# Gated linear attention with a mixture of adapters: the order and the rings of the input loads

## The chip, the cores and the metric

The kernel runs on one core of one Trainium2 chip. The metric is device time in microseconds (us) of one execution. Before the change three timed runs gave a median of 113.31 us (113.30 to 113.52). Five engines work side by side: TensorE (PE) for matmuls, VectorE (DVE), ScalarE (ACT), GpSimd (POOL) and SyncE (SP). Transfers between device memory and on-chip memory are issued as instructions on the SP or the ACT queue, each of which feeds a ring of its own, and are carried out by 16 DMA engines that both rings share.

## The reference

Two stages follow each other. The first is a recurrence over 768 time steps, for 4 batches of 8 heads, with a 48 by 48 state for each head:

```python
for t in range(S):
    state = alpha[:, :, t, :, None] * state + np.einsum('bhd,bhe->bhde', k[:, :, t], v[:, :, t])
    y[:, :, t] = np.einsum('bhd,bhde->bhe', q[:, :, t], state)
```

The second takes y as 3072 tokens of 384 features, picks the two best of eight experts for each token, and adds a rank-16 correction:

```python
logits = x @ w_gate                                   # 384 x 8
topk = np.argpartition(-logits, K, axis=1)[:, :K]     # K = 2
w = exp(sel - max) / sum                              # sel: the two chosen logits
delta[mask] += w[mask, k, None] * (x[mask] @ A[e]) @ B[e]
return x + delta
```

Inputs q, k, v and alpha are float32, 4 x 8 x 768 x 48 each: 4.72 MB each, 18.87 MB together. The adapter weights add 0.4 MB. The output is 4.72 MB.

## The kernel before

The time steps are cut into chunks of 128, so each batch has 6 chunks and there are 24 units (`NU`), numbered u = 6 b + c. One unit is 128 time steps on the partitions, with all 8 heads (384 numbers) along the row. Each input of one unit is one DMA of 192 KB (L290). In device memory a head's row is 48 floats, so this DMA is made of 1024 pieces of 192 bytes.

For one unit the work goes through these operations. The short names are those that the planner uses, and the line numbers are those of the profile.

- `ln` (L374, ACT): logarithm of alpha. Units 0 and 1 are done alone, then two units share one instruction (`LNS`), so `ln` of units 2 and 3 needs the alpha of both.
- `cum` (L379 to L385, PE): sums of the logarithms along time. `exp` (L390, ACT): their exponentials.
- `kg` (L395, POOL): k and q times the exponentials. `vb` (L403, POOL): v cast to bf16.
- `tr` (L409, PE): transposes. `kq` (L413, ACT): copy out of PSUM. `at` (L421, PE): scores. `msk` (L426, DVE): causal mask.
- `st` (L433, DVE) and `kv` (L441, L446, PE): the state carried from chunk to chunk. `av` (L456, L463, PE): the chunk's y. It needs `vb`.
- `ysb` (L468, ACT), `xt` (L481, PE), `xs` (L486, ACT): y copied out, transposed, copied out again.

Every three units (`GROUPS`; the last groups are [21, 22] and [23]) the adapter stage runs: `z` (L500, PE), the gate operations `gm`, `df`, `ge`, `gx`, `wu`, `dn`, `w` (L507 to L542, DVE but for `gx` on ACT), `zw` (L549, DVE), `zt` (L558, PE), `zs` (L564, ACT), and for each unit `dl` (L569, PE) and `o` (L577, DVE). The finished unit is stored by one DMA from SP (L600).

The order of instructions on each engine is fixed when the kernel is built. A list scheduler (`_order`) simulates the engines with assumed durations (`_ops`), assumed arrival times of the inputs (`_arrivals`) and a priority for each kind of operation (`PRIO`), and the instructions are written out in the order that it finds. On the chip each engine takes its instructions in that order and waits at each until its inputs are there.

The loads are ordered by `_plan`: for each unit alpha, k, q, v, in this order. `_ring` spreads them: of the first six the odd ones go to ACT, after that every fourth, which is always v. So SP carries 73 of the 99 loads (with the three weight loads) and ACT 26. SP issues nothing but DMAs. Its loads are written out by `pump`, and as SP does no other work it runs ahead until its ring has no room or a buffer is not free (each input has buffers for two batches, so the load for unit u needs the reading of unit u - 12 to be over). A load on ACT is an operation of the planner (`ld`), due `LEAD` = 5 us before its assumed arrival, and stands among ACT's other work, in order.

The weights are loaded on SP in a row, behind the first 20 input loads (L298 to L301). Three casts on DVE (`cast_weights`, L340 to L343) turn them into bf16. They are written out just before `xs` of unit 0. Stores are written out only once all loads have been.

Of the kernel before, what the change touches and what calls it, by code (L numbers as in the profile page):

```python
# [16 lines left out]
B, H, S, D = 4, 8, 768, 48  # L17
C = 128
# [14 lines left out]
LNS = [[0], [1]] + [[u, u + 1] for u in range(2, NU, 2)]  # L33
CAST = set()
LEAD = 5.
FIRST = 6


def _ring(i, item):
    return "ACT" if (i % 2 if i < FIRST else i % 4 == 3) else "SP"  # L40

def _act(n):
# [15 lines left out]
def _pe(t):  # L62
    return t + .22, t
# [2 lines left out]
SMALL = (.2, .09)  # L66
KEEP = dict(lg=2, ex=3, kg=4, kt=4, am=3, sb=2, vb=4, xs=9)
SLOTS = dict(C=1, A=1, M=3)
PRIO = dict(ln=-27.4, cum=-33.5, exp=14.2, kg=-6.0, vb=0.6, tr=4.7, kq=-8.2, at=6.7, msk=15.1,
            st=25.4, kv=6.9, av=-15.0, ysb=22.1, xb=5.9, xt=12.5, xs=-29.2, z=13.2, gm=32.7,  # L70
            df=16.8, ge=17.3, gx=21.3, wu=-9.0, dn=-22.2, w=39.9, zw=20.3, zt=1.9, zs=21.7,
            dl=6.9, o=21.2)
PERIOD = 2.0
SLACK = 0


def _plan():
    plan = []
    for u in range(NU):
        b, c = divmod(u, NCH)  # L80
        plan += [(x, b, c) for x in "akqv"]
    return plan


def _arrivals(plan):
    t, arr = 2.6, {}
    for i, (x, b, c) in enumerate(plan):
        t += 4.2 if c is None else .75
        for j in (range(NCH) if c is None else (c,)):
            arr[x, b * NCH + j] = t  # L90
        arr["due", i] = t - LEAD
    return arr


def _ops(arr):
    ops = {}

    def add(name, eng, length, deps, war=(), alloc=None, frees=None):
        ops[name] = (eng, length, list(deps), list(war), alloc, frees)

    gof = {u: g for g, us in enumerate(GROUPS) for u in us}
    lof = {u: us for us in LNS for u in us}
    prev = []
    for i, (x, b, c) in enumerate(_plan()):
        if i >= FIRST and _ring(i, (x, b, c)) == "ACT":
            war = []
            for j in (range(NCH) if c is None else (c,)):
                u = (b - 2) * NCH + j
                if u >= 0:
                    war.append(dict(a=("ln", lof[u][0]), k=("kg", u), q=("kg", u), v=("vb", u))[x])  # L110
            add(("ld", i), "ACT", (.5, .45), [("due", i)], war + prev)
            prev = [("ld", i)]
    for i, us in enumerate(LNS):
        war = [("cum", u) for u in LNS[i - KEEP["lg"]]] if i >= KEEP["lg"] else []
        add(("ln", us[0]), "ACT", _act(DM * len(us) + 30), [("a", u) for u in us], war)
    for u in range(NU):
        c = u % NCH
        p = u - KEEP["ex"]
        add(("cum", u), "PE", _pe(.49), [("ln", lof[u][0])], alloc="C")
        add(("exp", u), "ACT", _act(776), [("cum", u)],  # L120
            [("kg", p)] + ([("st", p)] if p % NCH else []), frees=("cum", u))
        p = u - KEEP["kg"]
        add(("kg", u), "POOL", _gp(768), [("exp", u), ("k", u), ("q", u)],
            [("tr", p)] + ([("kv", p)] if p % NCH < NCH - 1 else []))
        add(("vb", u), "POOL", _gpc(DM), [("v", u)], [("av", u - KEEP["vb"])])
        add(("tr", u), "PE", _pe(.48), [("kg", u)], alloc="M")
        add(("kq", u), "ACT", _act(512), [("tr", u)], [("av", u - KEEP["kt"])], frees=("tr", u))
        add(("at", u), "PE", _pe(.40), [("kq", u)], alloc="A")
        add(("msk", u), "DVE", _dve(1024), [("at", u)], [("av", u - KEEP["am"])], frees=("at", u))
        if c:  # L130
            add(("st", u), "DVE", _dve(DM), [("kv", u - 1), ("exp", u)], [("av", u - KEEP["sb"])])
        if c < NCH - 1:
            add(("kv", u), "PE", _pe(.33 if c else .17),
                [("vb", u), ("kg", u)] + ([("st", u)] if c else []),
                [] if c or not u else [("st", u - 1)])
        add(("av", u), "PE", _pe(.49 if c else .32),
            [("msk", u), ("vb", u), ("kq", u)] + ([("st", u)] if c else []), alloc="M")
        add(("ysb", u), "ACT", _act(DM), [("av", u)], frees=("av", u))
        if u in CAST:
            add(("xb", u), "POOL", _gpc(DM), [("ysb", u)])  # L140
            add(("xt", u), "PE", _pe(.17), [("xb", u)], alloc="M")
        else:
            add(("xt", u), "PE", _pe(.38), [("ysb", u)], alloc="M")
        p = u - KEEP["xs"]
        add(("xs", u), "ACT", _act(DM), [("xt", u)], [("z", gof[p])] if p >= 0 else [],
            frees=("xt", u))
    for g, us in enumerate(GROUPS):
        n = len(us)
        add(("z", g), "PE", _pe(.18 * n), [("xs", u) for u in us], alloc="M")
        add(("gm", g), "DVE", (.17 + .13 * (n - 1), .13 * n), [("z", g)])  # L150
        add(("df", g), "DVE", SMALL, [("gm", g)])
        add(("ge", g), "DVE", SMALL, [("gm", g)])
        add(("gx", g), "ACT", _act(E * n), [("df", g)])
        add(("wu", g), "DVE", SMALL, [("gx", g), ("ge", g)])
        add(("dn", g), "DVE", SMALL, [("wu", g)])
        add(("w", g), "DVE", (.4, .29), [("dn", g)])
        add(("zw", g), "DVE", _dve(P * n), [("w", g)], frees=("z", g))
        add(("zt", g), "PE", _pe(.057 * n), [("zw", g)], alloc="M")
        add(("zs", g), "ACT", _act(64 * n), [("zt", g)], frees=("zt", g))
        for u in us:  # L160
            add(("dl", u), "PE", _pe(.165), [("zs", g)], alloc="M")
            add(("o", u), "DVE", _dve(DM), [("dl", u)], frees=("dl", u))
    return ops
# [76 lines left out]
def kernel(  # L240
# [36 lines left out]
    def home(x, b):  # L277
        i = b % 2
        return dict(a=a_t[i], k=kq_t[i][:, 0], q=kq_t[i][:, 1], v=v_t[i])[x]

    def view(t):
        return t.rearrange("p (h c) d -> p c h d", h=H)[:, :, :, 0:D]

    def load(item, eng):
        x, b, c = item
        t, src = home(x, b), SRC[x][b]
        if c is None:
            eng.dma_start(out=t[:, :, 0:D], in_=src.rearrange("h (c j) d -> j (h c) d", j=C))
        else:
            eng.dma_start(out=view(t)[:, c],  # L290
                          in_=src[:, c * C:(c + 1) * C, :].rearrange("h j d -> j h d"))
# [5 lines left out]
    def load_weights():  # L297
        nc.sync.dma_start(out=W_st.rearrange("p e i r -> p e (i r)"),  # L298
                          in_=moe_A.rearrange("e (p i) r -> p e (i r)", i=NF))
        nc.sync.dma_start(out=G_st, in_=moe_w_gate.rearrange("(p i) e -> p i e", i=NF))  # L300
        nc.sync.dma_start(out=B_st, in_=moe_B.rearrange("e r f -> (e r) f"))  # L301

    queue = list(enumerate(plan))
    for i in range(FIRST):
        load(queue.pop(0)[1], nc.sync if _ring(i, plan[i]) == "SP" else nc.scalar)
    rings = {r: [x for x in queue if _ring(*x) == r] for r in ("SP", "ACT")}

    suf = consts.tile([P, P], F2, name="suf")
    nc.gpsimd.memset(suf, 1.0)
# [260 lines left out]
                         start=True, stop=True)  # L570

    def ld(i):
        assert rings["ACT"][0][0] == i
        load(rings["ACT"].pop(0)[1], nc.scalar)

    def o(u):
        nc.vector.tensor_tensor(out=o_t[u], in0=bank("dl", u)[:, 0:DM], in1=o_t[u], op=ALU.add)  # L577
# [6 lines left out]
    weights = 20  # L584
    done = []

    def pump(now):
        q = rings["SP"]
        while q:
            i, (x, b, c) = q[0]  # L590
            if arr["due", i] > now or any(
                    (b - 2) * NCH + j not in reads[x]
                    for j in (range(NCH) if c is None else (c,)) if b > 1):
                return
            load(q.pop(0)[1], nc.sync)

    def store(u):
        b, c = divmod(u, NCH)
# [2 lines left out]

    with tc.manual_schedule():
        for s, i in order:
            if (s, i) == ("xs", 0):
                cast_weights()
            RUN[s](i)
            for x, r in READ.items():
                if r == s:
                    for u in (LNS[lof[i][0]] if s == "ln" else (i,)):
                        reads[x].add(u)  # L610
            pump(when[s, i][0])
            if weights and len(plan) - len(rings["SP"]) - len(rings["ACT"]) >= weights:
                load_weights()
                weights = None
            if s == "o":
                done.append(i)
            if not rings["SP"] and not rings["ACT"]:
                while done:
                    store(done.pop(0))

# [29 lines left out]
```

## Time and profile before

| what | value |
|---|---|
| median of three timed runs | 113.31 us |
| the profiled execution's own time | 113.9 us |
| its span, first to last instruction | 112.2 us |
| mean granted TensorE clock | 0.906 of full speed |
| read from device memory / written | 19.28 MB / 4.72 MB |
| last alpha (unit 23) landed | 87.1 us |
| last load issued on SP | 83.63 to 86.27 us |
| first store issued, last `o` starts | 86.4 us, 108.7 us |

All times are microseconds from the first instruction of the profiled execution. Outside the span lie 1.7 us (113.9 less 112.2). The busy time of an engine is an average over stages with different limits, so the stretches from the profile that the prediction shows matter more than the totals. "Idle before, releaser" beside a group of instructions tells how long the engine stood still just before them and what it waited for. A name that ends in q (SPq, ACTq) is an engine's queue: the time that it spends on issuing a DMA is not counted as busy.

### The profile page before, as it was taken

Reading aid. Unit: us, or ns where it says so; the run is one execution under the profiler, and the core shown is the slowest. Engines: PE = TensorE matmul, PEld = TensorE weight load, DVE = VectorE, ACT = ScalarE, POOL = GpSimd, SP = SyncE. Lnnn points to the kernel's source line nnn. Section 1 sums busy time; section 2 is a strip of 40 time slices with the busy share of each in tenths; the row PEclk is TensorE's granted clock in tenths of the full one; section 3 lists DMA queues with packets and bytes.
Section 4 is the critical chain, followed back from the end, with each engine's and each line's share of the span. In section 5 each row is a group of like instructions: output and inputs, shape, how many; then the busy total and the mean of one; then the engine's idle time right before and its main releaser. Section 6 shows DMA issues by size and latency. Waiting matters only on the chain.

```text
span 112.2 us, 2916 instructions
## 1 busy us (share of the span) xinstructions
PE 80.6 (72%) x1112; PEld 62.2 (55%) x1112; DVE 69.1 (62%) x170; ACT 66.2 (59%) x128; POOL 56.2 (50%) x58
## 2 busy tenths in 40 slices
PE   0346994099995496978947969899395699996540
PEld 0124863067874286856836748579283478974210
DVE  4004330765595287899575396967289265998990
ACT  4244476046973767967818769696592745754310
POOL 5077418605949278492691676839287076000000
PEclk9999999558999999999997699999999656999975
DMA  2999999899999899999989999999899999013064
GB/s 57 259 259 259 259 230 275 181 224 212 247 240 185 165 256 237 220 244 205 230 173 214 256 241 187 246 243 229 175 259 191 338 394 390 9 72 141 3 235 186
DMA packets 104638, 24.19 MB, mean 216 GB/s; under 512 B 101424, under 2 KB 104624, under 8 KB 104624
## 3 DMA queue, kind: packets, MB, share of 16 engines
q1 hardware_dynamic: 77584, 18.89, 74.4%
q10 hardware_dynamic: 27040, 5.11, 22.7%
q8 instruction: 8, 0.13, 0.5%
q14 instruction: 6, 0.05, 0.2%
HBM read 19.28 MB, written 4.72 MB: 214 GB/s over the span
## 4 chain that ended last, share of the span: by engine, by line
SPq 39%; DMA 18%; PE 16%; DVE 16%; issue 4%; ACT 3%; DVEq 1%; POOL 1%; ACTq 0%; POOLq 0%
SPq L290 37%; DMA a_t<-in_alpha_dram 18%; DVE am L426 5%; DVE o_t L577 3%; ACT lg L374 3%; PE M_t L409 2%; PE cum_t L379 2%; DVE zw L549 2%; PE M_t L481 2%; DVE w L542 2%; PE at_t L421 2%; PE cum_t L380 1%; PE M_t L456 1%; SPq L300 1%; SPq L298 1%
## 5 line engine op out<-in xcount | busy, mean ns | idle before, releaser
L395 POOL TENSOR_TENSOR kgq<-kq_t,ex 128x768 bf16<-128x768 f32 x24 | 43.6, 1818 | 29.4 <-ACT ex L390 29.4
L426 DVE TENSOR_TENSOR am<-at_t,mask 128x1024 bf16<-128x1024 f32 x24 | 29.3, 1221 | 8.9 <-PE at_t L421 8.8
L390 ACT ACTIVATE ex<-cum_t 128x776 f32<-128x776 f32 x24 | 19.7, 822 | 5.8 <-PE cum_t L385 5.4
L379 PE MATMUL cum_t<-lg,suf 128*128 128x384 bf16 x24 | 9.0, 377 | 16.1 <-ACT lg L374 15.8
L374 ACT ACTIVATE lg<-a_t 128x768 bf16<-128x768 f32 (+1 forms) x13 | 10.3, 795 | 15.9 <-DMA a_t<-in_alpha_dram 15.9
L433 DVE TENSOR_TENSOR sb<-S_t,ex 128x384 bf16<-128x384 f32 x20 | 11.0, 551 | 13.1 <-PE S_t L446 8.7
L409 PE MATMUL M_t<-ident,kgq 128*128 128x128 bf16 x192 | 16.9, 238 | 2.7 <-POOL kgq L395 2.2
L413 ACT COPY kqt<-M_t 128x512 f32<-128x512 f32 x24 | 14.0, 584 | 8.0 <-PE M_t L409 7.7
L403 POOL CAST vb<-v_t 128x384 bf16<-128x384 f32 x24 | 12.0, 509 | 8.7 <-PE M_t L463 5.9
L409 PEld LDWEIGHTS <-kgq 128*128 128x128 bf16 x192 | 12.8, 107 | 4.9 <-POOL kgq L395 3.1
L577 DVE TENSOR_TENSOR o_t<-M_t,o_t 128x384 f32<-128x384 f32 x24 | 12.5, 551 | 3.6 <-PE M_t L569 3.4
L481 PE MATMUL M_t<-ident,o_t 128*128 128x128 f32 x72 | 14.1, 315 | 0.4 <-ACT o_t L468 0.4
L486 ACT CAST xs<-M_t 128x384 bf16<-128x384 f32 x24 | 11.2, 480 | 3.5 <-PE M_t L481 2.6
L468 ACT COPY o_t<-M_t 128x384 f32<-128x384 f32 x24 | 11.6, 483 | 1.9 <-PE M_t L463 1.9
L380 PEld LDWEIGHTS <-nsuf 128*128 128x128 bf16 x24 | 2.5, 105 | 15.5 <-issue 15.3
L481 PEld LDWEIGHTS M_t<-ident,o_t 128*128 128x128 f32 x72 | 10.2, 203 | 1.1 <-ACT o_t L468 0.9
L421 PE MATMUL at_t<-kqt 48*128 48x128 bf16 x192 | 10.6, 236 | 0.4 <-ACT kqt L413 0.4
L463 PE MATMUL M_t<-vb,am 128*128 128x48 bf16 x192 | 9.3, 189 | 0.3 <-DVE am L426 0.3
L446 PEld LDWEIGHTS <-kgq 128*128 128x128 bf16 x80 | 6.4, 110 | 5.2 <-issue 4.3
L380 PE MATMUL cum_t<-lg,nsuf 128*128 128x384 bf16 x24 | 9.2, 384 | 0.0
L441 PE MATMUL S_t<-sb,ident 128*128 128x384 bf16 x16 | 5.9, 370 | 3.5 <-DVE sb L433 3.5
L569 PE MATMUL M_t<-B_all,zs 128*128 128x384 bf16 x24 | 7.1, 338 | 1.3 <-DVE o_t L577 0.5
(47 smaller groups left out, 102.1 us busy)
## 6 DMA issues: line engine op xcount, KB each, us to landing
a_t<-in_alpha_dram SPq DMA_DIRECT2D x24, 192.0 KB, 4.3
kq_t<-in_q_dram SPq DMA_DIRECT2D x24, 192.0 KB, 4.4
v_t<-in_v_dram ACTq DMA_DIRECT2D x24, 192.0 KB, 4.0
out_dram<-o_t SPq DMA_DIRECT2D x24, 192.0 KB, 2.5
kq_t<-in_k_dram SPq DMA_DIRECT2D x22, 192.0 KB, 4.5
kq_t<-in_k_dram ACTq DMA_DIRECT2D x2, 192.0 KB, 4.3
W_st<-in_moe_A_dram SPq DMA_DIRECT2D x1, 192.0 KB, 4.6
B_st<-in_moe_B_dram SPq DMA_DIRECT2D x1, 192.0 KB, 4.0
```

The lines of the kernel that those rows point to most:

```text
L290: eng.dma_start(out=view(t)[:, c], in_=src[:, c * C:(c + 1) * C, :].rearrange("h j d -> j h d"))
L374: nc.scalar.activation(lgs[i % KEEP["lg"]][:, 0:n, :, 0:D], view(a_t[b % 2])[:, c:c + n], AF.Ln)
L380: nc.tensor.matmul(cum_t[:, N0:D0], nsuf[:, :], t[:, :, 0:D], start=True, stop=True)
L390: nc.scalar.activation(st["ex"][u], cum_t[:, U0:D0 + 2 * NP], AF.Exp)
L395: nc.gpsimd.tensor_tensor(out=kgq[u % KEEP["kg"]][:, :, :, 0:D], in0=src, in1=st["ex"][u][:, 0:2 * DM].rearrange("p (w h d) -> p w h d", w ...
L403: nc.gpsimd.tensor_copy(out=st["vb"][u], in_=view(v_t[b % 2])[:, c])
L409: nc.tensor.transpose(t[:, w, p, :], pair(kgq[u % KEEP["kg"]][:, w], p), ident[:, :])
L413: nc.scalar.copy(t, bank("tr", u)[:, :])
L421: nc.tensor.matmul(at_t[:, hh, p, :], kq[rows, 0, p, :], kq[rows, 1, p, :], start=True, stop=True)
L426: nc.vector.tensor_tensor(out=st["am"][u].rearrange("p a b t -> p (a b) t"), in0=at_t.rearrange("p a b t -> p (a b) t"), in1=_bc_mid(mask[ ...
L481: nc.tensor.transpose(t[:, i * P:(i + 1) * P], x[:, i, :], idn[:, :])
L577: nc.vector.tensor_tensor(out=o_t[u], in0=bank("dl", u)[:, 0:DM], in1=o_t[u], op=ALU.add)
```

## The change

The list of loads is reordered, spread over the rings in another way, and written out in another way. The order and priorities of all other work come from the same planner with other numbers.

- `_plan` now starts a0, k0, q0, a1, v0, k1, q1, a2, a3, v1. After that each unit brings k and q, each even unit u also alpha of units u + 2 and u + 3, then v of the unit. The four weight loads (A in two halves) follow unit 3. The v of units 22 and 23 are the last two loads.
- `_ring` is strict alternation: even places on SP, odd places on ACT, weights included. That is 50 loads on each. Of the 100, the first eight (`FIRST`) are written out ahead of all other work, four on each ring.
- An `ld` on ACT keeps its due time of 5 us before the assumed arrival. The planner now books 0.1 us of ACT for it instead of 0.45 us. The loads of SP that lie between are written out with it; `pump` is gone. A load writes out when the buffer's earlier reading has been written out.
- `cast_weights` is written out just before `z` of group 0 instead of `xs` of unit 0.
- Assumed arrivals start at 2.9 us and come every 0.77 us (0.4 us for a weight load), where they started at 2.6 us and came every 0.75 us. All `PRIO` numbers, some PE durations and `SLACK` (0.05 us instead of 0) are new.

```diff
-FIRST = 6
-def _ring(i, item):
-    return "ACT" if (i % 2 if i < FIRST else i % 4 == 3) else "SP"
+FIRST = 8
+def _ring(i):
+    return "ACT" if i % 2 else "SP"
...
-PRIO = dict(ln=-27.4, cum=-33.5, exp=14.2, kg=-6.0, vb=0.6, tr=4.7, kq=-8.2, at=6.7, msk=15.1,
-            st=25.4, kv=6.9, av=-15.0, ysb=22.1, xb=5.9, xt=12.5, xs=-29.2, z=13.2, gm=32.7,
-            df=16.8, ge=17.3, gx=21.3, wu=-9.0, dn=-22.2, w=39.9, zw=20.3, zt=1.9, zs=21.7,
-            dl=6.9, o=21.2)
+PRIO = dict(ln=-64.4, cum=-19.5, exp=15.9, kg=-34.5, vb=36.9, tr=-5.5, kq=18.9, at=0.3, msk=25.2,
+            st=17.2, kv=6.3, av=-46.4, ysb=38.7, xb=6.2, xt=35.6, xs=-33.5, z=16.2, gm=44.4,
+            df=23.7, ge=23.8, gx=22.6, wu=-24.6, dn=-0.6, w=-22.4, zw=15.5, zt=-8.7, zs=-7.1,
+            dl=8.4, o=21.5)
-SLACK = 0
+SLACK = 0.05
 def _plan():
-    plan = []
-    for u in range(NU):
-        b, c = divmod(u, NCH)
-        plan += [(x, b, c) for x in "akqv"]
-    return plan
+    plan = [("a", 0), ("k", 0), ("q", 0), ("a", 1), ("v", 0), ("k", 1), ("q", 1), ("a", 2), ("a", 3), ("v", 1)]
+    for u in range(2, NU):
+        plan += [("k", u), ("q", u)]
+        if u % 2 == 0 and u + 2 < NU:
+            plan += [("a", u + 2), ("a", u + 3)]
+        if u < NU - 2:
+            plan += [("v", u)]
+        if u == 3:
+            plan += [("w", 0), ("w", 1), ("w", 2), ("w", 3)]
+    return plan + [("v", NU - 2), ("v", NU - 1)]
 def _arrivals(plan):
-    t, arr = 2.6, {}
-    for i, (x, b, c) in enumerate(plan):
-        t += 4.2 if c is None else .75
+    t, arr = 2.9, {}
+    for i, x in enumerate(plan):
+        t += .4 if x[0] == "w" else .77
...
-            add(("ld", i), "ACT", (.5, .45), [("due", i)], war + prev)
+            add(("ld", i), "ACT", (.4, .1), [("due", i)], war + prev)
...
-        add(("cum", u), "PE", _pe(.49), [("ln", lof[u][0])], alloc="C")
+        add(("cum", u), "PE", _pe(.52), [("ln", lof[u][0])], alloc="C")
...
+    A_src = moe_A.rearrange("e (p i) r -> p e (i r)", i=NF)
+    WSRC = ((W_st[:, 0:4].rearrange("p e i r -> p e (i r)"), A_src[:, 0:4]),
+            (W_st[:, 4:8].rearrange("p e i r -> p e (i r)"), A_src[:, 4:8]),
+            (G_st, moe_w_gate.rearrange("(p i) e -> p i e", i=NF)),
+            (B_st, moe_B.rearrange("e r f -> (e r) f")))
+    loaded = 0
+    def load_next():
+        nonlocal loaded
+        x, u = plan[loaded]
+        eng = nc.sync if _ring(loaded) == "SP" else nc.scalar
+        loaded += 1
+        if x == "w":
+            eng.dma_start(out=WSRC[u][0], in_=WSRC[u][1])
+            return
+        b, c = divmod(u, NCH)
+        eng.dma_start(out=view(home(x, b))[:, c],
+                      in_=SRC[x][b][:, c * C:(c + 1) * C, :].rearrange("h j d -> j h d"))
+    while loaded < FIRST:
+        load_next()
...
     def ld(i):
-        assert rings["ACT"][0][0] == i
-        load(rings["ACT"].pop(0)[1], nc.scalar)
+        assert loaded <= i
+        while loaded <= i or (loaded < len(plan) and _ring(loaded) == "SP" and free(loaded)):
+            load_next()
+    def free(i):
+        x, u = plan[i]
+        return u < 2 * NCH or u - 2 * NCH in reads[x]
...
-            if (s, i) == ("xs", 0):
+            if (s, i) == ("z", 0):
                 cast_weights()
             RUN[s](i)
...
-            pump(when[s, i][0])
-            if weights and len(plan) - len(rings["SP"]) - len(rings["ACT"]) >= weights:
-                load_weights()
-                weights = None
             if s == "o":
                 done.append(i)
-            if not rings["SP"] and not rings["ACT"]:
+            if loaded == len(plan):
                 while done:
                     store(done.pop(0))
```

More of the change, by code (lines that the diff above doesn't have):

```diff
@@ L68 @@
 SLOTS = dict(C=1, A=1, M=3)
-PRIO = dict(ln=-27.4, cum=-33.5, exp=14.2, kg=-6.0, vb=0.6, tr=4.7, kq=-8.2, at=6.7, msk=15.1,
-            st=25.4, kv=6.9, av=-15.0, ysb=22.1, xb=5.9, xt=12.5, xs=-29.2, z=13.2, gm=32.7,
-            df=16.8, ge=17.3, gx=21.3, wu=-9.0, dn=-22.2, w=39.9, zw=20.3, zt=1.9, zs=21.7,
-            dl=6.9, o=21.2)
+PRIO = dict(ln=-64.4, cum=-19.5, exp=15.9, kg=-34.5, vb=36.9, tr=-5.5, kq=18.9, at=0.3, msk=25.2,
+            st=17.2, kv=6.3, av=-46.4, ysb=38.7, xb=6.2, xt=35.6, xs=-33.5, z=16.2, gm=44.4,
+            df=23.7, ge=23.8, gx=22.6, wu=-24.6, dn=-0.6, w=-22.4, zw=15.5, zt=-8.7, zs=-7.1,
+            dl=8.4, o=21.5)
 PERIOD = 2.0
-SLACK = 0
+SLACK = 0.05
 def _plan():
-    plan = []
-    for u in range(NU):
-        b, c = divmod(u, NCH)
-        plan += [(x, b, c) for x in "akqv"]
-    return plan
-def _arrivals(plan):
-    t, arr = 2.6, {}
-    for i, (x, b, c) in enumerate(plan):
-        t += 4.2 if c is None else .75
-        for j in (range(NCH) if c is None else (c,)):
-            arr[x, b * NCH + j] = t
+    plan = [("a", 0), ("k", 0), ("q", 0), ("a", 1), ("v", 0), ("k", 1), ("q", 1), ("a", 2), ("a", 3), ("v", 1)]
[8 more added lines that the diff above has]
+    return plan + [("v", NU - 2), ("v", NU - 1)]
+def _arrivals(plan):
+    t, arr = 2.9, {}
+    for i, x in enumerate(plan):
+        t += .4 if x[0] == "w" else .77
+        arr[x] = t
         arr["due", i] = t - LEAD
@@ L102, in _ops @@
     lof = {u: us for us in LNS for u in us}
[L103 to L110, printed above, removed]
-            add(("ld", i), "ACT", (.5, .45), [("due", i)], war + prev)
-            prev = [("ld", i)]
+    war, prev = [], []
+    for i, (x, u) in enumerate(_plan()):
+        if u >= 2 * NCH:
+            p = u - 2 * NCH
+            war.append(dict(a=("ln", lof[p][0]), k=("kg", p), q=("kg", p), v=("vb", p))[x])
+        if i >= FIRST and _ring(i) == "ACT":
+            add(("ld", i), "ACT", (.4, .1), [("due", i)], war + prev)
+            war, prev = [], [("ld", i)]
     for i, us in enumerate(LNS):
@@ L125, in _ops @@
         add(("vb", u), "POOL", _gpc(DM), [("v", u)], [("av", u - KEEP["vb"])])
-        add(("tr", u), "PE", _pe(.48), [("kg", u)], alloc="M")
+        add(("tr", u), "PE", _pe(.5), [("kg", u)], alloc="M")
         add(("kq", u), "ACT", _act(512), [("tr", u)], [("av", u - KEEP["kt"])], frees=("tr", u))
-        add(("at", u), "PE", _pe(.40), [("kq", u)], alloc="A")
+        add(("at", u), "PE", _pe(.43), [("kq", u)], alloc="A")
         add(("msk", u), "DVE", _dve(1024), [("at", u)], [("av", u - KEEP["am"])], frees=("at", u))
@@ L132, in _ops @@
         if c < NCH - 1:
-            add(("kv", u), "PE", _pe(.33 if c else .17),
+            add(("kv", u), "PE", _pe(.36 if c else .18),
                 [("vb", u), ("kg", u)] + ([("st", u)] if c else []),
                 [] if c or not u else [("st", u - 1)])
-        add(("av", u), "PE", _pe(.49 if c else .32),
+        add(("av", u), "PE", _pe(.5 if c else .33),
             [("msk", u), ("vb", u), ("kq", u)] + ([("st", u)] if c else []), alloc="M")
@@ L282, in view @@
         return t.rearrange("p (h c) d -> p c h d", h=H)[:, :, :, 0:D]
[L284 to L291, printed above, removed]
     W_st = consts.tile([P, E, NF, R], F4, name="W_st")
@@ L295 @@
     B_st = consts.tile([P, DM], F4, name="B_st")
[L297 to L306, printed above, removed]
+    A_src = moe_A.rearrange("e (p i) r -> p e (i r)", i=NF)
[17 more added lines that the diff above has]
+        load_next()
     suf = consts.tile([P, P], F2, name="suf")
@@ L583 @@
     reads = defaultdict(set)
-    weights = 20
     done = []
[L587 to L595, printed above, removed]
     def store(u):
@@ L608 @@
                 if r == s:
-                    for u in (LNS[lof[i][0]] if s == "ln" else (i,)):
-                        reads[x].add(u)
-            pump(when[s, i][0])
-            if weights and len(plan) - len(rings["SP"]) - len(rings["ACT"]) >= weights:
-                load_weights()
-                weights = None
+                    reads[x].update(LNS[lof[i][0]] if s == "ln" else (i,))
             if s == "o":
                 done.append(i)
-            if not rings["SP"] and not rings["ACT"]:
+            if loaded == len(plan):
                 while done:
```

## The prediction

> **What bounds the kernel now.** I read the page's tenths first, then stretches of the span, the transfers at finer grain, the waits, and the chain that ended last.
>
> ```profile
> DMA  2999999899999899999989999999899999013064
> GB/s 57 259 259 259 259 230 275 181 224 212 247 240 185 165 256 237 220 244 205 230 173 214 256 241 187 246 243 229 175 259 191 338 394 390 9 72 141 3 235 186
> PEclk9999999558999999999997699999999656999975
> q8 instruction: 8, 0.13, 0.5%
> HBM read 19.28 MB, written 4.72 MB: 214 GB/s over the span
> ```
>
> Up to 87 us the DMA engines look full, but bytes move at 259 GB/s only in the first 14 us. Then the slices swing between 165 and 275. The stretches (columns: busy time by engine, granted clock, DMA share, GB/s):
>
> ```profile
> 4.00:14.00 10.00, 6.53 (x64) 4.74 (x64) 1.97 (x3) 4.46 (x8) 5.46 (x6) 1.00 1.28 259
> 20.00:40.00 20.00, 14.47 (x212) 11.21 (x212) 12.09 (x26) 11.89 (x22) 11.00 (x12) 0.85 1.04 208
> 40.00:60.00 20.00, 15.76 (x259) 12.78 (x256) 15.26 (x30) 14.23 (x29) 13.26 (x12) 1.00 1.11 219
> 60.00:80.00 20.00, 17.46 (x257) 14.01 (x256) 14.28 (x35) 14.24 (x29) 13.17 (x11) 0.91 1.14 229
> 88.00:94.00 6.00, 5.99 (x57) 4.55 (x57) 2.95 (x8) 3.14 (x6) 3.13 (x3) 0.50 1.07 396
> 94.70:109.30 14.60, 10.84 (x140) 7.37 (x135) 13.83 (x45) 6.60 (x18) 0.27 (x1) 0.96 0.28 102
> ```
>
> No compute engine is full before 88 us. The kernel is paced by its loads until then, and afterwards works off a backlog: PE at half clock (0.50), then DVE, 13.83 us busy in 14.60. The transfers from 30 to 40 us, in slices of 0.25 us:
>
> ```profile
> GB/s 259 260 258 259 260 254 234 253 308 217 210 237 210 209 235 248 252 261 244 125 35 55 157 245 248 125 16 41 151 234 259 188 108 158 170 237 257 250 248 258
> q8 instruction: 1, 0.02, 0.9%
> ```
>
> The rate falls to 16 GB/s, a sixteenth of 259: one of the 16 engines works and 15 stand still. Queue q8 had one packet of 16 KB here, 0.9% of 16 engines for 10 us, so 1.4 us on one engine. I read this as one engine held up by that packet, while the ring has no room for the others. The page has eight such packets. By the trace's packet records seven lie before 87 us and took 7.65 us in all. What a full ring does is seen on SP's queue (start, duration):
>
> ```profile
> 0.80 0.43 SPq L290 DMA_DIRECT2D a_t<-in_alpha_dram  x1
> ...
> 2.71 1.47 SPq L290 DMA_DIRECT2D kq_t<-in_q_dram  x1
> 4.22 1.47 SPq L290 DMA_DIRECT2D a_t<-in_alpha_dram  x1
> ```
>
> And on ACT's queue, beside ACT's own work:
>
> ```profile
> 29.06 0.58 ACT L413 COPY kqt<-M_t 128x512 f32<-128x512 f32 x1
> 29.07 0.37 ACTq L290 DMA_DIRECT2D v_t<-in_v_dram  x1
> ```
>
> An issue takes about 0.4 us with room, and 1.47 us when it must wait for some (half of 259 GB/s moves 192 KB in 1.52 us). On ACT an issue of 0.37 us hides entirely beside the copy that is running. The longest waits for transfers (total, times, longest), and then the chain at the last load:
>
> ```profile
> ACT lg L374 <- DMA a_t<-in_alpha_dram: 15.9, 10, 2.7
> DVE W L340 <- DMA W_st<-in_moe_A_dram: 4.4, 1, 4.4
> ```
>
> ```profile
> 81.28 5.81 DMA a_t<-in_alpha_dram
> 87.11 0.85 ACT lg L374
> ```
>
> ACT stands ten times before a pair's logarithm until its second alpha is there, and everything behind it in order waits too. The last such alpha is issued at 81.28, lands at 87.09, and from there a whole unit pair has still to run: 112.2 - 87.1 = 25.1 us.
>
> **The change, part by part.** The sum is made on the profiled execution: 113.9 us, span 112.2, 1.7 outside; the median of the three runs lies 0.6 below, at 113.3.
>
> *End of the loads.* Bytes stay the same. SP loses 23 issues (73 to 50), ACT gains 24 (26 to 50). Best case, both rings hold work throughout as from 4 to 14 us: 19.28 MB / 259 GB/s = 74.4 us from a start at 2, so 76.4. Worst case, nothing helps: SP's last q landed at about 87.9. Between lies the bound by one engine: if the 7.65 us of q8 fall on the same engine each time, no depth of rings recovers them: 2 + 74.4 + 7.65 = 84.1. I take 84.1, since the stalls with one engine active look like that case; gain 3.8 us.
>
> The Trainium skill, page "DMA: Bandwidth & Descriptors", section "Issuing engines are not separate DMA queues", speaks against a gain: all rings run on the same 16 engines, and a second issuer saves only issue time. By it the loads would end at 87.9 as now, and the sum would be 3.8 us more. The 259 against 208 GB/s are on the side of a gain, though the first stretch also had less compute beside it.
>
> *Alpha ahead.* Alpha of units 22 and 23 is now followed by ten loads (v20, k21, q21, v21, k22, q22, k23, q23, v22, v23). At (84.1 - 2)/100 = 0.82 us each it lands 8.2 us before the end. The 15.9 us of ACT waits should nearly go. What is late next is q: `kg` needs k and q, which now always lie on different rings, then ACT's `kq`.
>
> *v last.* `vb` (0.51) is needed only by `kv` and `av`, so the last v, 1.6 us behind q23, is hidden by `kg` (1.82), `tr`, `kq`, `at` and `msk`. Without that cover it costs at most the 1.6.
>
> *The tail.* From q23, 1.6 us before the loads' end E: `kg` 1.82, `tr` 0.5, `kq` 0.58, `at` 0.5, `msk` 1.22, `av` 0.55, `ysb` 0.48, `xt` 0.65, `xs` 0.48, `z` 0.35, gate about 1.75, `zw` 0.29, `zt` 0.25, `zs` 0.21, `dl` 0.35, `o` 0.55, with 15 hand-overs of 0.06 (the planner's figure): 11.4, so `o` ends at E + 9.8. Behind the last `o` (ends 109.3) stand 2.9 us for store and end. Floor: E + 12.7. Ceiling: today's 112.2 - 87.9 = 24.3. Work of DVE left after E: three `msk` 3.7, two `st` 1.1, six `o` 3.3, three `zw` 1.3, three gates 3.2 = 12.6 us, against 17.4 now from 87 to 109.3. As it must share with the chain I take 16.5, nearer the floor, because cum and exp of the last pair (now 88 to 93, at half clock) are done before E; gain 7.8.
>
> On the clock the row is 0.50 from 88 to 94 us with PE busy 5.99 of 6. The page "TensorE: Matmul & The Clock Gate", Part 1, says that an idle window of about 3.4 us halves the clock and as long a busy one restores it. By it a tail entered without a PE gap keeps full clock, one entered after a gap loses about 3 us. The trace has the half clock behind PE's gaps at 20 and 86 us.
>
> *ACT's issues.* Forty-six stand among its work. With room, 0.37 us beside a running instruction: nothing to 46 x 0.37 = 17 us, on an engine that is busy 66.2 of 112.2. I take nothing, by the row at 29.07, since the loads pace ACT. The first four now stand before the first `ln`: 0.48 + 0.69 + 1.20 as now, and one more of up to 1.47, so the first `ln` moves from 3.91 to about 4.8. Hidden by the loads; without that cover 0.9.
>
> *Stores.* They follow SP's loads and no longer all loads. If SP runs ahead, some 11 to 15 stores of 0.5 us (15 in 7.7 us from 86.36) compete with ACT's last loads, q22, q23, v23. From 0 to 7.7 us; I take 1.0, since both rings should end close together.
>
> *Weight casts.* DVE's wait of 4.4 us goes; it cost nothing, `msk` had none ready. The casts (1.28 + 0.18 + 0.36 = 1.8 us) now stand right before `z` of group 0, where PE waits for them with `tr`, `at` behind: 0 to 2 us at about 25, hidden by the loads. *Planner numbers*: order only; its effect lies in the bounds of the tail.
>
> Sum: -3.8 + 1.0 - 7.8 = -10.6. 113.9 - 10.6 = 103.3 in a profiled execution, 102.7 against the median.
>
> **Rivals.** *Late ACT ring.* ACT's loads are held by its compute, SP runs free, and kg is paced by the later ring. For: from 6 to 86 us, by the packet records, ACT's ring moved data in only 36 of 80 us. Against: five microseconds of lead are 6.5 loads, 3.2 on each ring, more than a full ring. Price: stores in the way 5 more, so 104 to 109.
>
> *Loads hidden from the change.* They end at 87.9 and the tail falls only to 19 to 22: 87.9 + 20.5 + 1.1 = 109.5 (108 to 112). For: the skill's rule and the single engine's bound.
>
> *ACT held by its issues: slower.* If the ring is mostly full when ACT issues, each takes 1.47 as on SP, of which 0.4 hides: 46 x 1.07 = 49 us on top of 66.2 busy, before any wait for PE. It decides once mean exposed holding passes about 0.8 us: 46 x 0.8 + 66.2 = 103, with 4 us of start and 5 of end. Then 114 to 125. Against: a held ACT issues later, and so finds more room.
>
> **How the numbers follow.** Forecast 0.57 (its own range 97 to 107); late ring 0.17; loads unchanged 0.10; ACT held 0.14; no change 0.02. A measurement here tells about 0.2%. Faster 0.84, same 0.02, slower 0.14. Low end 97: loads at 81, tail 15, 1.1 outside by the median. High end 112 takes in the first two rivals and leaves out ACT held.
>
> **What would show it.** Right: GB/s near 240 from 20 to 80 us, SP and ACT loads landing in turn, `lg` waits under 4 us, the last load near 84, PEclk over 0.9 in the tail. Wrong: ACTq issues of 1 us and more with POOL and PE waiting for ACT; stores before the last q; rates near 220 with both rings full.

## The result and the profile after

The changed kernel takes 121.42 us (median of four runs, 120.73 to 123.33), the kernel before 113.31 us on the same chip (four runs, 112.75 to 113.52). The ratio is 1.070, with a 95% interval of 1.061 to 1.080. It is slower by about 8 us, where 10.6 us less were forecast. The profiled execution took 120.78 us, with a span of 119.1.

The page's tenths of the kernel after:

```profile
DMA  3999999999998999999999897798699894031054
GB/s 56 259 259 254 210 243 259 248 187 259 259 259 174 194 258 260 256 251 207 248 257 263 280 250 142 159 290 166 137 249 203 162 249 122 0 135 63 3 216 180
```

Slices of 250 GB/s and more, which before were few after 14 us, now come again and again up to the 24th slice (71 us). Then the rate breaks: 142, 159, 166, 137. The stretches (columns: busy time by engine, granted clock, DMA share, GB/s):

```profile
20.00:40.00 20.00, 11.52 (x154) 9.09 (x152) 7.58 (x19) 8.95 (x18) 10.15 (x9) 0.88 1.11 229
40.00:60.00 20.00, 15.83 (x184) 12.01 (x184) 10.18 (x21) 11.20 (x22) 7.48 (x8) 0.69 1.21 243
60.00:80.00 20.00, 15.61 (x241) 12.46 (x237) 12.78 (x29) 12.84 (x24) 11.41 (x10) 0.91 0.99 235
80.00:98.00 18.00, 17.62 (x293) 14.44 (x290) 16.85 (x40) 16.50 (x34) 14.70 (x13) 1.00 0.87 194
100.00:119.00 19.00, 10.74 (x134) 7.12 (x130) 14.44 (x43) 6.61 (x18) 1.75 (x3) 0.86 0.26 95
```

From 20 to 60 us more bytes arrive than before (229 and 243 GB/s against 208 and 219) and yet the engines do less: DVE is busy 17.8 us in these 40, before 27.4. So the bytes that arrive are not the ones that are wanted next. SP issues its last load at 62.5 us, when ACT has issued 29 of its 50. SP's stores begin at 63.2, ACT alone brings the remaining 21 loads, and the last packet of the last one lands at 99.8 us (before: 88.3). The end of the loads is taken from that packet here and below. The waits for transfers, in the list of waits (total, times, longest):

```profile
ACT o_t L468 <- DMA v_t<-in_v_dram: 5.9, 3, 4.7
...
ACT zs L564 <- DMA kq_t<-in_k_dram: 4.4, 1, 4.4
...
ACT lg L374 <- DMA a_t<-in_alpha_dram: 2.9, 1, 2.9
```

The waits for alpha have gone from 15.9 to 2.9 us, as forecast. The two other rows make no sense as data: L468 and L564 copy from PSUM and read neither v nor k. ACT's rows in time order show what stands in front of such a copy (start, duration, in brackets the idle time before it):

```profile
34.64 0.82 ACT L390 ACTIVATE ex<-cum_t 128x776 f32<-128x776 f32 x1 [0.37 <-PE cum_t L385]
39.39 0.46 ACTq L302 DMA_DIRECT2D v_t<-in_v_dram  x1
39.90 0.32 ACT L564 COPY zs<-M_t 128x192 f32<-128x192 f32 x1 [4.43 <-DMA kq_t<-in_k_dram]
```

It is a load that ACT itself has to issue. The issue takes 0.46 us, but it begins only at 39.39, and a load of k that SP had issued at 33.65 landed at 39.37. The instructions of the built program explain the pair. Each transfer, of either ring, is given one of eight completion semaphores (counters that tell when a transfer has landed), in turn. The instruction that issues it first waits, on its own engine, until the transfer eight places earlier has landed; SP's loads wait so too. The framework numbers the transfers by a simulated time of its own, in which SP, with nothing else to do, runs up to 22 loads ahead. So eight places before a load of ACT's there is often one of SP's that has hardly left. Some of ACT's loads, from the program and the records of landing (places counted from 0):

| place, load of ACT | eight places earlier | that landed | ACT issued | ACT held |
|---|---|---|---|---|
| 42, q | 34, ACT alpha | 29.06 | 29.36 | 0 |
| 51, v | 43, SP k | 39.37 | 39.39 | 4.75 |
| 66, q | 58, SP v | 50.76 | 50.78 | 1.82 |
| 69, alpha | 61, SP k | 54.10 | 54.12 | 1.78 |
| 85, k | 77, SP v | 67.44 | 67.46 | 5.17 |

"Held" is the time from the start of ACT's instruction before it to the issue, where the issue follows the landing within 0.15 us; up to 0.8 us of one lies beside that instruction. In the changed kernel 26 of ACT's 50 loads wait for a transfer of SP's in this way, and these holds come to 29.4 us. Before it was 3 of 26 and 2.0 us: there 12 loads follow a transfer of SP's, but nine of these are alphas, and the program has no such wait behind them. The Trainium skill, page "DMA: Bandwidth & Descriptors", section "Anatomy of one DMA — SWDGE (gpsimd) path", says that a wait on a semaphore is made by the issuing sequencer before dispatch and never by the DMA engines. The section is about transfers that GpSimd issues; the pairs of the table agree for those of ACT. In the chain that ended last the pairs stand one behind another:

```profile
48.45 5.64 DMA kq_t<-in_k_dram
54.12 0.46 ACTq L302
...
63.20 4.77 DMA out_dram<-o_t
67.98 0.62 ACTq L302
```

### The profile page after: what moved, and what is told of

Its sections match the earlier page's. It is cut to its first block, busy times and chain, and to the rows that moved or that the text cites. A ratio compares the mean times of both kernels' runs of the same rounds, so it can differ in the third digit from the quotient of the medians.

```text
span 119.1 us, 2908 instructions
## 1 busy us (share of the span) xinstructions
PE 83.1 (70%) x1112; PEld 64.1 (54%) x1112; DVE 68.5 (58%) x170; ACT 66.3 (56%) x128; POOL 56.1 (47%) x58
## 4 chain that ended last, share of the span: by engine, by line
PE 30%; DMA 19%; SPq 18%; DVE 16%; ACT 6%; issue 3%; ACTq 2%; POOL 2%; DVEq 0%; POOLq 0%
SPq L302 16%; DMA v_t<-in_v_dram 8%; PE M_t L409 5%; DMA kq_t<-in_k_dram 5%; PE M_t L481 5%; DMA out_dram<-o_t 4%; DVE am L426 3%; DMA kq_t<-in_q_dram 3%; DVE o_t L582 3%; PE at_t L421 3%; PE M_t L456 2%; PE M_t L569 2%; PE cum_t L379 2%; PE M_t L463 2%; ACTq L302 2%
## 5 line engine op out<-in xcount | busy, mean ns | idle before, releaser
L390 ACT ACTIVATE ex<-cum_t 128x776 f32<-128x776 f32 x24 | 19.7, 822 | 6.8 <-PE cum_t L385 4.2
L481 PE MATMUL M_t<-ident,o_t 128*128 128x128 f32 x72 | 15.5, 330 | 4.5 <-ACT o_t L468 4.5
L409 PE MATMUL M_t<-ident,kgq 128*128 128x128 bf16 x192 | 17.4, 244 | 1.4 <-POOL kgq L395 1.4
L468 ACT COPY o_t<-M_t 128x384 f32<-128x384 f32 x24 | 11.5, 478 | 8.2 <-DMA v_t<-in_v_dram 5.9
L409 PEld LDWEIGHTS <-kgq 128*128 128x128 bf16 x192 | 13.9, 111 | 2.9 <-POOL kgq L395 1.7
L481 PEld LDWEIGHTS M_t<-ident,o_t 128*128 128x128 f32 x72 | 10.8, 204 | 5.8 <-ACT o_t L468 5.1
L421 PE MATMUL at_t<-kqt 48*128 48x128 bf16 x192 | 10.6, 236 | 4.3 <-ACT kqt L413 4.2
L569 PE MATMUL M_t<-B_all,zs 128*128 128x384 bf16 x24 | 8.0, 372 | 5.4 <-ACT zs L564 4.9
L421 PEld LDWEIGHTS <-kqt 48*128 48x128 bf16 x192 | 6.0, 101 | 7.2 <-ACT kqt L413 5.3
L380 PE MATMUL cum_t<-lg,nsuf 128*128 128x384 bf16 x24 | 9.8, 406 | 0.0
L456 PE MATMUL M_t<-sb,kqt 128*128 128x96 bf16 x80 | 7.5, 223 | 1.8 <-ACT kqt L413 1.6
L463 PEld LDWEIGHTS <-am 128*128 128x128 bf16 x192 | 7.8, 103 | 1.3 <-DVE am L426 1.2
(47 smaller groups left out, 94.9 us busy)
```

The source lines that it names most:

```text
L390: nc.scalar.activation(st["ex"][u], cum_t[:, U0:D0 + 2 * NP], AF.Exp)
L409: nc.tensor.transpose(t[:, w, p, :], pair(kgq[u % KEEP["kg"]][:, w], p), ident[:, :])
L421: nc.tensor.matmul(at_t[:, hh, p, :], kq[rows, 0, p, :], kq[rows, 1, p, :], start=True, stop=True)
L463: nc.tensor.matmul(y[:, h * D:(h + 1) * D], st["am"][u][:, hh, p, :], st["vb"][u][:, h, :], start=(c == 0 and h == 0), stop=(h == H - 1), ...
L481: nc.tensor.transpose(t[:, i * P:(i + 1) * P], x[:, i, :], idn[:, :])
```

## The experiments

The theory S is that ACT, with all its compute behind, is held at its loads until older transfers of SP's have landed, and that the holds make ACT's loads late. Its main rival (B in the later texts) is that SP's running ahead costs by itself, because its loads take the bytes that ACT's loads need. The kernels of one table below ran on the same chip with their own runs of the kernel before, where the text doesn't say otherwise.

**One part alone, and the opposite of it.** Four kernels:

```diff
 # v on ACT: the changed kernel, 3 of 4 loads on SP
-    return "ACT" if i % 2 else "SP"
+    return "ACT" if (i % 2 if i < FIRST else _plan()[i][0] == "v") else "SP"
 # alternate only: the kernel before, strict alternation and ACT's 0.1 us alone
-    return "ACT" if (i % 2 if i < FIRST else i % 4 == 3) else "SP"
+    return "ACT" if i % 2 else "SP"
 # all on SP: the changed kernel, ACT loads only among the first eight;
 # SP's loads are written out at their due times
-    return "ACT" if i % 2 else "SP"
+    return "ACT" if i < FIRST and i % 2 else "SP"
 # in step: the changed kernel, each load of SP's waits for ACT's five places ahead
+    if i >= FIRST and _ring(i) == "SP":
+        tc.add_manual_dep(sent[i].ins, sent[i - 5].ins.name, ...)   # has landed
```

> The changed kernel with the rings of before: behind the first eight loads only v is issued on ACT, all else on SP. The new order of loads and the new planner numbers stay. Theory S (ACT stands at its own load issues, because each first waits until the transfer that last used the same completion semaphore, mostly a young SP load, has landed; the trace of the changed kernel has 29.3 us of this): with 27 loads on ACT instead of 50 these waits fall under 8 us, the time to 104 to 113 us. Theory P (the new order of compute work from the planner is at fault): still 117 us or more. Theory R (half of the loads on ACT's ring is too many, whatever the semaphores do): falls as under S.

> The kernel before with strict alternation of the rings alone (and ACT's booking of 0.1 us that goes with it); its order of loads and planner priorities stay. Theory S: 23 of its 48 loads on ACT follow an SP transfer on their semaphore, so ACT stands 20 us and more there; 117 to 125 us. Theory P: the fault is not in it; 112 to 114 us. Theory R: 117 us or more.

> The changed kernel with every load behind the first eight on SP, in the new order, none among ACT's work. Theory S: ACT's waits at issues are gone; one ring moves 208 to 230 GB/s, so the loads end at 86 to 92 us, and the early alphas shorten what follows; 104 to 112 us. Theory P: 117 us or more.

> The changed kernel with strict alternation kept, but each SP load waits until the ACT load five places before it has landed, so that SP can't run ahead; ACT's instructions and their order stay as they are. The semaphore that an ACT load waits for was then last used by an older load, mostly ACT's own. Theory S: ACT's waits at issues fall from 29.3 to under 8 us, both rings stay fed, the loads end at 84 to 90 us; 103 to 112 us. Theory R: ACT has as many issues as before, so 117 us or more. Theory P: 117 us or more.

| kernel (before: 111.28 us) | median us | ratio, interval | ACT held | last load |
|---|---|---|---|---|
| v on ACT | 115.03 | 1.032, 1.021 to 1.043 | 16.1 | 94.2 |
| alternate only | 125.07 | 1.127, 1.118 to 1.136 | 29.1 | 97.3 |
| all on SP | 116.34 | 1.048, 1.039 to 1.056 | 1.8 | 96.7 |
| in step | 101.72 | 0.915, 0.903 to 0.927 | 1.1 | 81.2 |

Alternation alone gives the kernel before the same 29 us of holds and costs it 13.8 us. Keeping SP in step takes 17 to 20 us from the changed kernel, although it adds waits (19.7 by the medians of two chips, some 17 by the ratios 1.070 and 0.915). It leaves ACT's order of work and its number of loads as they are, so neither the new order (theory P) nor the half of the loads on ACT (theory R) was the cause of the loss. The stretches of the kernel in step:

```profile
20.00:40.00 20.00, 17.45 (x274) 13.66 (x271) 15.57 (x38) 15.57 (x31) 13.29 (x12) 1.00 1.24 251
...
60.00:80.00 20.00, 17.98 (x290) 14.70 (x288) 18.64 (x40) 16.31 (x32) 15.33 (x14) 1.00 1.25 261
```

Two of the four I missed: v on ACT and all on SP came out slower than their texts said. All on SP has no holds to speak of, yet its loads end at 96.7. One ring by itself is slower:

```profile
20.00:40.00 20.00, 14.60 (x213) 11.21 (x211) 14.12 (x30) 11.58 (x23) 10.97 (x9) 0.91 1.00 197
...
60.00:80.00 20.00, 16.42 (x239) 13.13 (x238) 13.99 (x29) 12.59 (x24) 12.03 (x11) 0.91 1.03 204
```

So two things are needed, both rings fed and ACT not held. V on ACT has neither: 214 to 224 GB/s, and 16.1 us of holds, of which 3.0 and 3.5 us fall on its last two held loads, issued at 86.1 and 90.1.

**A dose, and the old order.** SP may run 7, 15 or 31 places ahead instead of 5; and the kernel before with alternation, in step.

```diff
-        tc.add_manual_dep(sent[i].ins, sent[i - 5].ins.name, ...)
+        tc.add_manual_dep(sent[i].ins, sent[i - 7].ins.name, ...)   # or 15, or 31
 # old order in step: the kernel "alternate only", and in its load()
+        if i >= 8 and _ring(i, item) == "SP":
+            tc.add_manual_dep(sent[i].ins, sent[i - 5].ins.name, ...)
...
```

> Like the run in step, but each of SP's loads waits for ACT's load seven places ahead of it in the order of loads, not five. Theory S (ACT stands at a load until an older transfer of SP's on the same semaphore has landed; the built order of transfers decides how often): 9 of ACT's 50 loads now follow a transfer of SP's on their semaphore (5 in step, 26 in the changed kernel), hold 1 to 4 us, 101.5 to 104 us. Rival B (SP's loads that run ahead take the bytes that ACT's loads need, and the hold is only a sign of it): one load of 0.77 us more ahead, 102 to 103. The two do not part here; it is the first step of a dose.

> The same with 15 places: SP may run 7 loads ahead of ACT. In the built order the rings still alternate one by one from the 30th transfer on, so that eight back is mostly the same ring: 13 of 50 follow SP. Theory S: hold 3 to 8 us, nearly all before 30 us, 102 to 106 us. Rival B: the loads that ACT brings arrive up to 7 x 0.77 = 5.4 us later than in step, 106 to 109 us, with the last load landing near 87.

> The same with 31 places: SP may run 15 loads ahead, nearly as far as in the changed kernel (19). 17 of 50 follow SP on their semaphore. Theory S: hold 6 to 14 us, 104 to 111 us. Rival B: 15 x 0.77 = 11.6 us late and SP's stores ahead of ACT's last loads, 113 to 118 us, near the changed kernel's 119 or so.

> The kernel before, its order of loads (alpha, k, q, v of a unit) and its planner's numbers, with the rings alternating and SP in step (five places). Theory O (the order of the change is worth what the prediction said: the waits for alpha and a tail of 24 us stay): loads end near 82 as in step with the new order, tail 22 to 25, 105 to 109 us, ACT waiting 10 us and more before its logarithms. Rival F (all that matters is that both rings are fed): 101 to 103 us. If above 112, the planner's numbers of before do not fit alternating rings at all.

The kernel before took 111.86 us beside them, with runs from 108.79 to 113.23, so these carry no ratio; their own runs lie within 2%. The first row and the row "free" are the runs from above, on other chips. SP's lead is the loads of SP that have landed by 60 us, less those of ACT; the tail is the span less the landing of the last load.

| places SP may run ahead | SP's lead | ACT held | last load | tail | median us |
|---|---|---|---|---|---|
| 5 | 0 | 1.1 | 81.2 | 18.4 | 101.72 |
| 7 | 1 | 9.1 | 83.6 | 17.9 | 103.84 |
| 15 | 5 | 14.5 | 88.7 | 19.9 | 110.36 |
| 31 | 13 | 22.9 | 94.8 | 19.3 | 115.39 |
| free (the changed kernel) | 20 | 29.4 | 99.8 | 19.3 | 121.42 |
| 5, old order | 3 | 10.6 | 83.9 | 24.8 | 110.43 |

Time follows the holds, but the lead grows with them, so the totals don't part S and B. 15 places came out above what either had said, 31 places inside B's range. I had judged the holds too small from the number of loads that follow SP.

The places where time is lost say more. With 15 places, ACT is held 7.3 us by three loads before 14 us, then 0.3, 0.4 and 0.8 us, then nothing until 72 us, then 1.3, 3.4 and 1.0 us. Against the run with seven places, `kg` starts 2.6 us later at unit 3 (19.2 us), 3.7 at unit 6, 4.1 at unit 19 (71.7) and 9.4 at unit 21 (83.4). So it loses time at the start and at the end, where the holds are, and hardly any in the 47 us between. This alone doesn't refute B: SP leads by four to six loads all the while, and under B a steady lead means a steady delay.

In the changed kernel the holds show one by one. Against the run in step, the start of its `kg` falls behind in steps. From unit 3 to 4 it loses 3.4 us (the hold before 23.34 is 3.28), from unit 7 to 8 4.9 (4.75 before 39.39), from unit 9 to 10 3.7 (1.82 and 1.78 before 50.78 and 54.12), and from unit 12 to 13 3.7 (5.17 before 67.46). From there on, with no hold over 0.2 us, it stays 18.6 to 21.3 us behind to the end. SP gains its lead in the same time, so a lead without holds stays unpriced: no run has one with both rings fed, or gives each ring semaphores of its own, which would part the two directly. Nor does every hold cost: with seven places ACT is held 3.5 us by four loads before 14 us, and the starts of `kg` up to unit 8 lie within 0.3 us of those with five.

With seven places, where SP leads by one or two loads, a single hold can be followed. Until unit 20 this kernel is ahead of the one with five, by 1.9 us in the start of `kg` of unit 17. Then, in ACT's rows:

```profile
76.26 0.82 ACT L400 ACTIVATE ex<-cum_t 128x776 f32<-128x776 f32 x1
79.86 0.38 ACTq L304 DMA_DIRECT2D v_t<-in_v_dram  x1
80.27 0.48 ACT L478 COPY o_t<-M_t 128x384 f32<-128x384 f32 x1 [3.19 <-DMA out_dram<-o_t]
```

ACT's last load stands 3.6 us behind a store of SP's on its semaphore, and `kg` of unit 23 starts 2.1 us behind that of the other kernel. A hold costs here with next to no lead.

The old order in step fits theory O in the tail, but is 1.4 us over its range in time, and its waits for alpha, 5.2 us, are half of what the text said. It isn't free of holds (10.6 us), so its time is not that of the order alone.

**Stores, casts and the planner's numbers.**

```diff
 # stores behind: in store(), on the changed kernel and on the one with seven places
+        tc.add_manual_dep(s.ins, sent[-1].ins.name, ...)   # ACT's last load has landed
 # casts early: seven places, stores behind, and
-            if (s, i) == ("z", 0):
+            if (s, i) == ("xs", 0):
 # old planner numbers: seven places, stores behind, PRIO of before and
-SLACK = 0.05
+SLACK = 0
```

> The changed kernel, SP's first store waiting until ACT's last load has landed (no store beside a load, and no load of ACT's behind a store on a semaphore). Theory S: the loss is made by 68 us, at ACT's holds behind SP's loads; in the changed kernel only 0.1 us of hold stands behind a store. So at most 3 us of the 121.4 go, and the 24 stores that now wait for the last load (about 0.55 us each, 18 of them ready) cost nothing more, since they leave while the tail computes: 117 to 122 us. Rival T (the stores take the bytes that ACT's last 19 loads need): 15 stores of 0.77 us beside the loads, 10 us back: 108 to 113 us.

> In step with seven places, and SP's first store waiting until ACT's last load has landed. In the run with seven places alone, the second last load of ACT's but one stood 3.60 us at 79.86 behind a store on its semaphore, and from there each unit was 2.1 us later than with five places, after having been up to 2 us earlier. Theory S: that single hold goes, the last load lands near 80, and the time falls by 2 to 4 us, to 99.5 to 102 us, at or below the run with five places (101.7). Rival B (no hold matters by itself): 103 to 104.5 us as with seven places alone.

> The run with seven places and stores behind, but the casts of the weights back where they stood before (ahead of the first group's xs, not of its z). The prediction took 0 to 2 us near 25 us, hidden by the loads. With them early DVE stands at W_st until it lands (4.4 us in the kernel before). If hidden: within 1.0 us of the run with the casts late, either way. If DVE's wait is now on the path, since the loads run ahead of compute: 1 to 4 us slower.

> The run with seven places and stores behind, its new order of loads, but the planner's priorities and slack of the kernel before. The kernel before's order and numbers in step took 110.4. If the order of the loads (alpha ahead, v last) is what makes the short tail: within 2 us of the run with the new numbers, 100 to 104 us. If the planner's numbers carry it: 106 to 111 us. Half and half: 104 to 106.

| kernel (before: 112.26 us) | median us | ratio, interval | ACT held | last load | tail |
|---|---|---|---|---|---|
| changed kernel, stores behind | 116.75 | 1.031, 1.019 to 1.042 | 23.3 | 94.9 | 22.1 |
| seven places, stores behind | 98.67 | 0.882, 0.876 to 0.888 | 4.9 | 78.6 | 17.7 |
| the same, casts early | 100.21 | 0.897, 0.891 to 0.902 | 4.9 | 80.8 | 19.3 |
| the same, old planner numbers | 102.47 | 0.915, 0.907 to 0.924 | 5.1 | 79.5 | 21.5 |

Holding back the stores gives the changed kernel some 4.7 us (medians of two chips, whose runs scatter by 2 to 3%), a little more than S said and less than half of what rival T said. The holds fall by 6.1 us, since the load of k that stood 5.17 us at 67.46 no longer does. (The profile of this kernel is of an execution of 118.78 us, above its median.)

With seven places it gives 5.2 us (medians of two chips), more than the 2 to 4 of its text, and the fastest kernel of the study, 12% faster than the kernel before. Rival B had none of this gain. Its `kg` starts as in the run with seven places alone up to unit 21 (73.8 against 74.0), and that of unit 23 at 77.8 instead of 81.6. The store that held ACT accounts for 3.6 us; the rest may be the stores that moved beside ACT's last two loads there. SP's first store, which waits for the last load, is issued at 78.98 us. From the page:

```profile
PEclk9999999999999999999999999999999999999755
...
GB/s 31 254 259 259 259 259 257 251 259 259 259 252 252 236 252 258 254 256 259 256 259 260 257 258 258 259 257 259 260 258 259 258 96 246 389 391 392 135 280 131
```

From the second slice to the 32nd it never moves less than 236 GB/s, and the clock is full until the last three slices.

Early casts cost 1.5 us: DVE stands 1.6 us for the first weights and 1.1 us for the last, at 16 to 20 us, and from unit 6 on `kg` starts 1.8 to 2.3 us later (in an execution of 101.80 us, above the median). The planner's old numbers cost 3.8 us, more than the 2 us that I had put on them; they stand in the tail (21.5 against 17.7). Of the 7.1 us between the tail of the old order in step (24.8) and that of the fastest kernel, the planner's numbers then have 3.8 and the order of the loads at most the other 3.3; the two kernels between which the 3.3 stands also differ in places, casts and stores.

## Why the prediction was wrong, by its own steps

- **"ACT's issues ... I take nothing"** is the step that failed. It priced an issue by the room in the ring, 0.37 to 1.47 us, and bounded 46 of them by 17 us. The issues did stay short (median 0.40 us of the 46, the longest 1.41). What it left out is the wait ahead of an issue: 29.4 us, beyond its upper bound. In the profiled execution the sum missed by 17.5 us (120.8 against 103.3): 15.7 in the end of the loads and 2.8 in the tail, less the 1.0 for stores. The trace of before has this wait, at 8.06 us, where ACT issues a v 0.02 us after a q of SP's has landed. With 2.0 us in all it was easy to pass over.
- **"Stores: I take 1.0, since both rings should end close together."** They ended 33 us apart: SP's last load at 67.0 us, ACT's at 99.8. The term is about 4.7 us by the run with the stores held back, inside the 0 to 7.7.
- **The end of the loads, 84.1.** In the changed kernel it is 99.8, because of the holds. With both rings fed and holds under 5 us it is 78.6 to 81.2, better than taken. The argument for 84.1, that the 16 KB packets of q8 hold one engine and no depth of rings recovers that, doesn't hold: the packets are there in all runs, and of the 7.7 us down to the best case of 76.4 the fastest kernel recovers 5.5. The 87.9 that the term starts from is the landing of the last k; the last q of before ends at 88.3.
- **Alpha ahead.** Right: 15.9 to 2.9 us, and 3.6 in the fastest kernel.
- **The tail of 16.5.** Right in direction, too short by 1.2 to 2.8 us: 17.7 in the fastest kernel, 19.3 in the changed one, 24.8 with the old order and numbers. *Planner numbers* as "order only" fell short, since they carry 3.8 of it.
- **What would show it.** PEclk over 0.9 in the tail was missed: 0.86 from 100 to 119 us, and 0.82 from 80 to 96 in the fastest kernel. GB/s near 240 came true (229 to 243) in a kernel that got slower: a rate doesn't tell whose bytes arrive.
- **Weight casts, hidden.** Off by 1.5 us: with the loads no longer the pace, the late casts are a gain.
- **Rival "Late ACT ring"** named the place (SP free, ACT's ring late, stores in the way), and was dismissed because five microseconds of lead time were more than a full ring. Lead time in ACT's order of work is worth nothing while ACT stands still. It priced the stores alone, 5 us, and not the late loads themselves.
- **Rival "ACT held by its issues"** has the sign and the range (114 to 125). Its mechanism, the full ring at 1.47 us an issue, is not what happened, and its threshold does not hold either: it was to decide at a mean hold of 0.8 us, and the mean here is 29.4 / 50 = 0.59. ACT did not become the bound; its late loads did.

With nearly all holds gone, the changed order takes 101.72 us, and 98.67 with the stores behind as well. That the first lies so near the forecast of 102.7 is in part luck: its loads end 2.9 us sooner than taken (81.2), its tail is 1.9 us longer (18.4), and it has waits that the change hasn't.

## What to carry to other kernels

Before loads are given to an engine that computes, look for what its issue instruction waits on, not only for how long the issue takes: here the completion semaphore eight transfers back, used by both rings. A compute instruction that waits, by the profile, for a transfer it doesn't read stands behind such an issue. Keep a ring that runs free in step with one that doesn't, and keep stores out of the order until the last load of the computing engine is out; two added waits turned a loss of 7% into a gain of 12%.

## What the runs showed of the hardware

With two fed rings the rate doesn't fall behind a packet as it does with one. The 16 KB packets of q8 are in all profiles, eight in each, 0.88 to 1.60 us long. The transfers in slices of 0.25 us behind one of them, first with all loads on SP (30 to 40 us, the packet from 29.4 to 30.3), then in the fastest kernel (27 to 37 us, the packet from 28.7 to 29.6):

```profile
GB/s 194 147 55 18 14 20 143 220 257 166 85 101 200 213 235 260 261 232 197 181 196 230 218 244 220 206 217 246 210 202 193 185 210 237 260 222 172 181 222 222
```

```profile
GB/s 260 237 241 241 234 254 322 240 244 243 247 252 254 253 260 260 260 257 263 262 204 194 227 204 246 257 260 247 243 250 247 243 260 256 263 258 259 257 258 257
q8 instruction: 1, 0.02, 0.5%
```

With one ring the rate falls to 14 GB/s, with two it stays above 190. By the packet records it falls to about 100 GB/s or less (11 at the lowest) behind each of the seven packets among the loads of the first, and behind none of the six from 28 to 71 us in the second. That may be part of why one ring moves 197 to 204 GB/s in 192-byte pieces from 20 to 80 us and the two in step 251 to 261. No run without the packets shows how large a part; with all on SP, SP also waited 9.4 us before its loads until other engines had done. The page "DMA: Bandwidth & Descriptors", section "Issuing engines are not separate DMA queues", says that issuing on several engines saves only the time of the issue; the end of the loads, 78.6 us with two rings and 96.7 with one, says otherwise for these loads. Whether it is the depth of the second ring alone, or also the way in which an engine takes turns between rings, no run here tells.
